# A second routing search of eight rounds with an exactness test, a branch of VectorE alone, and bounds brought into rows by VectorE

## The chip, the cores and the metric

The kernel runs on one core of a Trainium2 chip. Its engines are TensorE (matmuls, in the profile PE, its weight loads PEld), VectorE (DVE), ScalarE (ACT), GpSimd (POOL, here also the queue of gathers and scatters) and SyncE (SP, the queue of all other transfers). The metric is the device time of one execution in microseconds, lower is better; the profile adds one execution taken with the hardware profiler.

## What is computed

Block-causal attention over 8 batches, 8 heads and 576 positions, whose output, as 4608 rows of 512, goes through a mixture of 8 experts. Each expert takes exactly 576 rows, in the order of all logits together:

```python
logits = x @ w_gate                      # 4608 x 8
order = np.argsort(-logits.flatten())
for idx in order:
    tok, e = (int(idx) // E, int(idx) % E)
    if assigned[tok] >= 0 or counts[e] >= cap:
        continue
    assigned[tok] = e
    counts[e] += 1
for e in range(E):
    mask = assigned == e
    out[mask] = np.maximum(x[mask] @ w1[e], 0.0) @ w2[e]
```

The kernel gets the same assignment in eight searches. In each, every row that is left proposes to its best expert that is left; for every expert the 576th largest proposal is found; the expert for which it is highest wins, takes its 576 rows, and both drop out.

## The kernel before

The first half, class Attn, computes the attention and the logits. The second, class Moe, has three kinds of work per expert, all written as generators. `route(k)` is search k: which expert is the k-th, and which rows it takes. `weights(k)` loads that expert's weights on SyncE's queue (L1018) and splits them into two 16-bit parts (ScalarE L1035, L1042, L1046; GpSimd L1048, or VectorE L1037 for part of the first two experts). `gather(k)` fetches the rows by index on GpSimd's queue (L1078); they are turned by a DMA transpose (L1104), those of the first expert by TensorE (L1089). `ffn(k)` is the two layers: h (L1129) in two stretches of rows, each with eight blocks (h_0 to h_7), evacuated by ScalarE into HH (L1115) and by VectorE into HL (L1117); then y (L1155, L1159) in five blocks of rows, y_0 to y_4, evacuated by ScalarE (L1137) and scattered to the output on GpSimd's queue (L1145).

A search (L735 on) narrows a lower bound for every expert in base 4. All proposals lie as PB, one expert to each group of partitions (partition number modulo 8). In round t three candidates per expert are tried, 1, 2 and 3 steps of 4^-t above the bound. VectorE counts the proposals below two of them (L801), ScalarE those of the third by a sum of signs (ja, L770); a small matmul adds the counts over the partitions of one expert (tot, L817); VectorE turns the sums into the next digit (sg, L820). Behind round six the proposals are shifted by the bound (P2, L774), so that later digits keep their precision. After 14 rounds (`NS`) `finish()` adds the last digit (L825, L826); TensorE transposes the bounds, which lie one expert to a partition, into rows that every partition sees (th L831, bc L832); VectorE finds the winner (L835 to L845, the one-hot row oh), its bounds and the rows above them (L849 to L861). `place` numbers the rows by prefix sums and matmuls (po, L903 to L907), `invert` makes a list of indices of them (pe L1005, ps L1012, ix L1014).

The first search (k = 0) already does four rounds only (`NX`), then a test (L885 to L897) whose result TensorE, ScalarE, VectorE and SyncE load into a register (L975). If it is not zero they skip the rounds 4 to 13 (L962).

The order of every engine's instructions is fixed when the program is built: class Sched keeps the generators as tasks, with a cost, a priority and conditions for each step, and lists the step that can start first. Engines run their lists in that order and wait for semaphores, so a matmul that waits for VectorE holds all matmuls behind it. Conditions that matter here: `route(k)` starts when search k-1 is done and y_0 of expert k-2 has begun (`('mid',k-2)`); `gather(k)` waits until expert k-2 is done. Accumulators of h and y are four banks (tag "g"). Index lists, expert numbers and weights hang on the end of a search: `weights(k)` is started from L859, `gather(k)` behind ix.

Of the kernel before, what the change touches and what calls it, by code (L numbers as in the profile page):

```python
# [625 lines left out]
class Moe:  # L626
    def __init__(s,tc,nc,ctx,sc,L,xd,w1,w2,out):
        s.tc,s.nc,s.sc,s.L,s.xd,s.w1,s.w2,s.out=tc,nc,sc,L,xd,w1,w2,out
        s.NT=xd.shape[0]; s.D=w1.shape[1]; s.E=w1.shape[0]; s.F=w1.shape[2]; s.CAP=s.NT//s.E; s.C=s.NT//P
        s.NS=14; s.NSC=6; s.NX=4  # L630
        s.IFE=(mybir.EngineType.Activation,mybir.EngineType.PE,mybir.EngineType.DVE,mybir.EngineType.SP)
        s.cp=ctx.enter_context(tc.tile_pool(name="mcp",bufs=1))
        s.ident=s.cp.tile([P,P],F32,name="mident"); make_identity(nc,s.ident)
        s.am=s.cp.tile([P,8],F32,name="m_am"); s.nam=0; nc.gpsimd.memset(s.am,2.0**-50)
        s.ab=s.cp.tile([P,1],F32,name="m_ab")
        s.vm=s.cp.tile([P,s.C],F32,name="m_vm"); s.nP=s.cp.tile([P,s.C,s.E],F32,name="m_nP"); s.Lr=s.cp.tile([P,s.C,s.E],F32,name="m_Lr")
        s.early=[]; s.W={}; s.X={}; s.ix={}; s.half={}; s.ny=0
# [38 lines left out]
    def pools(s,ctx):  # L676
# [52 lines left out]
    def route(s,k):  # L729
        nc=s.nc; rp=s.rp; C,E=s.C,s.E; V=nc.vector; sc=s.sc  # L730
# [18 lines left out]
        else:  # L749
            if k==0: PB,PV,CB,base=s.first  # L750
            else:
# [11 lines left out]
                CB,base=s.begin(k); sc.busy(D,250)  # L763
# [15 lines left out]
            lo=CB[:,0:1]; nw=s.zero; PBx=PB; wk=s.wk if k else s.sw  # L779
            BC=s.BC[k%2]; f=rp.tile([P,3,8],F32,tag="f",name=f"f{k}"); m1=rp.tile([P,6],F32,tag="m1",name=f"m1{k}"); oh=f[:,1]  # L780
            los,lo2s,hi2s,ei=[m1[:,i:i+1] for i in range(2,6)]; d2=R("d2"); u=rp.tile([P,8],F32,tag="u8",name=f"u8{k}")
            def rounds(t0,t1,live):
                nonlocal lo,nw,PBx,base
                for t in range(t0,t1):
                    w=4.0**-t
                    cnt=rp.tile([P,3],F16,tag="cnt",name=f"cn{k}_{t}")
                    cand=base
                    if t:
                        cand=rp.tile([P,3],F32,tag="cand",name=f"cd{k}_{t}")
                        yield D,70 if k==0 else 210,('P2',k) if PBx is not PB else None  # L790
                        if k==0: V.tensor_tensor(cand[:,2:3],base[:,2:3],nw,op=OP.add)
                        else:
                            for i in (2,0,1): V.tensor_scalar(cand[:,i:i+1],lo,nw,(i+1)*w,op0=OP.add,op1=OP.add)
                    P2=s.P2 if t==s.NSC else None
                    sg=signs(PBx,cand[:,2:3],cnt,t,P2)
                    if live: sc.add(sg,0,sc.now+200); sc.nolat()
                    for i in range(2):
                        yield D,429
                        jk=rp.tile([P,N],F16,tag="jk",name=f"jk{k}_{t}_{i}")
                        if t and k==0: V.scalar_tensor_tensor(jk,base[:,i:i+1].to_broadcast([P,N]),nw,PBx[:,:N],op0=OP.add,op1=OP.is_gt,accum_out=cnt[:,i:i+1])  # L800
                        else: V.tensor_scalar(jk,PBx[:,:N],cand[:,i:i+1],0.0,op0=OP.is_lt,op1=OP.add,accum_out=cnt[:,i:i+1])  # L801
                        if i==0 and live: sc.nolat()
                    add=lambda o,a,b: V.tensor_tensor(o,a,b,op=OP.add) if k==0 else V.tensor_scalar(o,a,b,None,op0=OP.add)
                    if t: add(lo,lo,nw)
                    if P2 is not None:
                        V.tensor_scalar(CB[:,2:3],lo,-1.0,None,op0=OP.mult); sc.set(('nlo',k))
                        lo=CB[:,1:2]; PBx=P2
                    if not live:
                        for _ in sg: pass
                    if t==s.NS-1: add(CB[:,2:3],CB[:,0:1],lo)  # L810
                    elif k==0:
                        base=rp.tile([P,3],F32,tag="base",name=f"bs{k}_{t}")
                        V.tensor_scalar(base,s.io3,wk[:,t+1:t+2],lo,op0=OP.mult,op1=OP.add)
                    if live: sc.busy(D,330 if k==0 else 150)
                    yield T,30,('sg',k,t)
                    tot=s.ps.tile([P,512],F32,tag="tot",name=f"tot{k}_{t}")
                    nc.tensor.matmul(tot[:,0:3],lhsT=s.bo,rhs=cnt,start=True,stop=True)  # L817
                    yield D,72
                    sg=rp.tile([P,4],F32,tag="sg",name=f"sg{k}_{t}")
                    V.scalar_tensor_tensor(sg[:,0:3],tot[:,:3],s.NT-s.CAP+0.5,wk[:,t:t+1].to_broadcast([P,3]),op0=OP.is_le,op1=OP.mult,accum_out=sg[:,3:4])  # L820
                    nw=sg[:,3:4]
                    if live: sc.lag(93)
            def finish():
                yield D,140
                V.tensor_scalar(CB[:,2:3],CB[:,2:3],nw,None,op0=OP.add)  # L825
                V.tensor_scalar(lo,lo,nw,None,op0=OP.add)  # L826
                yield T,90,'rt'
                tk=sc.take()
                ps=s.ps.tile([P,512],F32,tag="rt",name=f"bc{k}")
                th=s.ps.tile([P,512],F32,tag="tot",name=f"th{k}")  # L830
                nc.tensor.transpose(th[:,:32],CB[:32,2:3].to_broadcast([32,P]),s.ident[:32,:32])  # L831
                for i in range(2): nc.tensor.transpose(ps[:,32*i:32*i+32],CB[:32,i:i+1].to_broadcast([32,P]),s.ident[:32,:32])  # L832
                th=th[:,0:8]
                yield D,77
                V.tensor_reduce(m1[:,0:1],th,axis=AX.X,op=OP.max)  # L835
                yield D,138
                V.scalar_tensor_tensor(f[:,0],th,m1[:,0:1],s.wt8,op0=OP.is_equal,op1=OP.mult)
                pb=ps[:,:64].rearrange("p (i x) -> p i x",i=2)[:,:,0:8]
                if k: V.tensor_copy(BC[:,0:2],pb); V.tensor_scalar(BC[:,2],ps[:,32:40],4.0**(1-s.NS),None,op0=OP.add)
                else: V.tensor_scalar(BC[:,0:2],pb,s.gr,None,op0=OP.mult); V.tensor_scalar(BC[:,2],ps[:,32:40],s.gr,4.0**(1-s.NS),op0=OP.mult,op1=OP.add)  # L840
                sc.set(tk)
# [7 lines left out]
                V.tensor_tensor(sm,BC,oh[:,None,:].to_broadcast([P,4,8]),op=OP.mult)  # L849
                V.tensor_tensor(d2,PV,be(oh),op=OP.mult)  # L850
                yield D,670
                V.tensor_reduce(m1[:,2:6],sm,axis=AX.X,op=OP.add)
                V.tensor_reduce(ds_,d2,axis=AX.X,op=OP.add)
                yield D,420
                V.tensor_scalar(MM[:,0],ds_,los,hi2s,op0=OP.subtract,op1=OP.is_gt)
                ge=rp.tile([P,C],F16,tag="ge",name=f"ge{k}")
                V.tensor_scalar(ge,ds_,los,lo2s,op0=OP.subtract,op1=OP.is_ge)
                V.tensor_copy(eidx,ei)
                if k: sc.add(s.weights(k,eidx),1,sc.now)  # L859
                yield D,106  # L860
                V.tensor_tensor(MM[:,1],ge,MM[:,0],op=OP.subtract)  # L861
            if k:
                yield from rounds(0,s.NS,True)
                yield from finish()
            else:
                yield from rounds(0,s.NX,True)
# [356 lines left out]
```

## Time and profile before

| | us |
|---|---|
| median of 3 runs (770.09 to 771.24) | 771.02 |
| the profiled execution | 771.09 |
| its span, first to last instruction | 769.3 |
| TensorE busy in the span | 715.6 |
| VectorE busy | 559.4 |
| ScalarE busy | 536.6 |
| GpSimd busy | 467.8 |

Rows of the timeline and of groups read: start (or none), busy time, engine, line, operation, output<-inputs, shapes, count; in square brackets the engine's idle time before the row and what ended it. Groups end in total busy time, mean nanoseconds of one, and idle time before them. The attention takes the first 340 us. The first expert's layers begin at 361, the second's at 418.5; each later one takes about 50.

### The profile page before, as it was taken

What the parts mean: (1) busy time and instruction counts of PE and PEld (TensorE: products, weight loads), DVE (VectorE), ACT (ScalarE), POOL (GpSimd) and SP (SyncE); (2) the same over time, 40 slices, a digit from 0 to 9 for tenths busy, and PEclk for the clock granted to TensorE, in tenths of its full rate; (3) what the DMA queues carried; (4) which work ended last, traced back from release to release, by engine and by line L of the source; (5) the groups of instructions that cost most, each with busy time, mean ns of one, the idle gap of its engine ahead of it and who ended that gap; (6) DMA issues with size and microseconds to landing.
All of it is one profiled execution on the core that took longest, in us unless ns stands there. A gap on an engine that the chain in (4) does not pass through costs nothing.

```text
span 769.3 us, 19008 instructions
## 1 busy us (share of the span) xinstructions
PE 715.6 (93%) x6516; PEld 474.7 (62%) x6516; DVE 559.4 (73%) x2290; ACT 536.6 (70%) x1451; POOL 467.8 (61%) x515
## 2 busy tenths in 40 slices
PE   5879999999999999966999999999999999999997
PEld 3557776766776777743545747647567475574753
DVE  6899889997799888758988978879687693430210
ACT  5788888988898898844935869594965948393211
POOL 5888978997799876714314448293761926666001
PEclk9999999999999999986999999999999999999999
DMA  9888999999999995266229376482925719853101
GB/s 203 163 160 171 207 187 216 201 168 226 187 210 171 221 196 103 78 124 192 99 74 228 104 247 158 161 211 71 292 76 193 178 43 268 273 139 88 35 14 49
DMA packets 249122, 122.84 MB, mean 160 GB/s; under 512 B 205600, under 2 KB 232096, under 8 KB 249024
## 3 DMA queue, kind: packets, MB, share of 16 engines
q1 hardware_dynamic: 243088, 102.60, 60.2%
q0 software_dynamic: 5936, 19.01, 7.9%
q8 instruction: 52, 0.85, 0.5%
q14 instruction: 46, 0.38, 0.2%
HBM read 71.45 MB, written 18.87 MB: 117 GB/s over the span
## 4 chain that ended last, share of the span: by engine, by line
PE 40%; DMA 5%; issue 4%; POOL 3%; ACT 1%; POOLq 0%; SPq 0%; DVE 0%; ACTq 0%; DVEq 0%
PE h L1129 22%; PE y L1155 15%; DMA raw<-in_moe_w_dram 2%; PE y L1159 2%; POOL xg L1078 2%; POOL W L1048 1%; DMA X<-xg 1%; DMA out_dram<-yo,ix 1%; PE pe L1005 1%; ACT ja L770 1%; DMA xg<-x,ix 0%; PE tot L817 0%; ACT yo L1137 0%; POOL out_dram L1145 0%; ACT raw L1042 0%
## 5 line engine op out<-in xcount | busy, mean ns | idle before, releaser
L442 POOL TENSOR_TENSOR P<-P,m 128x320 f32<-128x320 f32 (+8 forms) x285 | 210.2, 773 | 46.0 <-DVE m L434 30.6
L1129 PE MATMUL h<-X,W 128*128 128x320 f16 (+3 forms) x1536 | 195.4, 286 | 1.6 <-DMA X<-xg 1.6
L1129 PEld LDWEIGHTS <-W 128*128 128x128 f16 x1536 | 141.5, 98 | 43.1 <-issue 3.7
L420 ACT ACTIVATE P<-psb,m 128x576 f32<-128x576 f32 (+8 forms) x288 | 149.7, 548 | 25.6 <-DVE m L413 17.7
L1155 PE MATMUL y<-W,HH 128*128 128x512 f16 x512 | 152.3, 379 | 0.0
L409 DVE TENSOR_REDUCE m<-psb 128x1 f32<-128x576 f32 (+8 forms) x288 | 124.9, 481 | 11.6 <-PE psb L384 11.3
L1048 POOL TENSOR_TENSOR W<-raw,W 128x1024 f16<-128x1024 f32 x56 | 118.3, 2134 | 19.7 <-ACT W L1046 17.3
L467 PE MATMUL psb<-mident,P 128*128 128x128 f32 x800 | 104.6, 278 | 10.4 <-POOL P L442 5.4
L1145 POOL DMA_INDIRECT out_dram<-yo,ix x40 | 39.2, 981 | 118.0 <-ACT yo L1137 73.0
L384 PEld LDWEIGHTS <-qT 128*64 128x64 f16 x1408 | 77.0, 111 | 42.3 <-issue 28.0
L384 PE MATMUL psb<-kT,qT 128*64 128x288 f16 (+8 forms) x704 | 90.8, 284 | 10.8 <-ACT P L420 9.5
L467 PEld LDWEIGHTS psb<-mident,P 128*128 128x128 f32 x800 | 86.3, 141 | 22.0 <-POOL P L442 8.2
L502 PE MATMUL psb<-PT,V 128*64 128x448 f32 (+5 forms) x776 | 97.2, 388 | 0.9 <-DVE PT L450 0.4
L1155 PE MATMUL y<-W,HL 128*128 128x512 f16 x256 | 97.0, 379 | 0.0
L1115 ACT ACTIVATE HH<-h 128x320 f16<-128x320 f32 (+3 forms) x128 | 52.0, 410 | 62.3 <-PE h L1129 57.1
L1078 POOL DMA_INDIRECT xg<-x,ix x40 | 40.9, 1022 | 81.4 <-DMA raw<-in_moe_w_dram 48.5
L448 ACT ACTIVATE PT<-psb 128x512 f32<-128x512 f32 (+1 forms) x165 | 82.7, 595 | 5.3 <-PE psb L467 5.0
L1117 DVE SCALAR_TENSOR_TENSOR HL<-h,HH 128x320 f16<-128x320 f32 (+3 forms) x128 | 57.3, 452 | 37.0 <-ACT HH L1115 36.6
L384 PE MATMUL psb<-kS,qT 128*64 128x288 f16 (+8 forms) x704 | 83.2, 281 | 0.4 <-DVE kS L354 0.2
L1155 PEld LDWEIGHTS <-HH 128*128 128x128 f16 x512 | 46.9, 98 | 52.9 <-issue 1.8
L1042 ACT ACTIVATE raw<-raw 128x512 f32<-128x512 f32 x112 | 67.7, 625 | 9.4 <-DMA raw<-in_moe_w_dram 9.4
L502 PEld LDWEIGHTS psb<-PT,V 128*64 128x64 f32 x776 | 49.5, 137 | 32.2 <-issue 24.3
(241 smaller groups left out, 1035.3 us busy)
## 6 DMA issues: line engine op xcount, KB each, us to landing
raw<-in_moe_w_dram SPq DMA_DIRECT2D x64, 512.0 KB, 5.3
x<-XR SPq DMA_DIRECT2D x8, 1152.0 KB, 5.6
kn<-in_k_dram SPq DMA_DIRECT2D x15, 576.0 KB, 5.0
qn<-in_q_dram SPq DMA_DIRECT2D x15, 576.0 KB, 7.2
V<-in_v_dram SPq DMA_DIRECT2D x64, 128.0 KB, 4.1
V<-in_v_dram SPq DMA_DIRECT2D x16, 64.0 KB, 3.6
xg<-x,ix POOLq DMA_INDIRECT x41, 4.5
out_dram<-yo,ix POOLq DMA_INDIRECT x40, 2.8
```

The source lines that it names most:

```text
L384: nc.tensor.matmul(out if len(K1.shape) == 2 else out.rearrange("p (r j) -> p r j", r=2), lhsT=A[:, h, 64 * i:64 * i + 64], rhs=K1, start= ...
L409: nc.vector.tensor_reduce(m[:, 0, c:c + 1], ps[:, o:o + 64 * (i + 1)] if g else s.part(ps, g, i, o), axis=AX.X if g else AX.XY, op=OP.max)
L420: nc.scalar.activation(out, in_, AF.Exp, bias=m[:, 1, c:c + 1], scale=s.ESC, accum_out=m[:, 2, c:c + 1])
L442: nc.gpsimd.tensor_tensor(sl, sl, m[:, 3, c:c + 1].to_broadcast([P, w]), op=OP.mult)
L448: s.nc.scalar.activation(out, in_, AF.Copy)
L467: nc.tensor.transpose(ps[:, a], s.Pb[n % s.NP][:, s.OFF[i] + 128 * j:s.OFF[i] + 128 * j + P], s.ident)
L502: nc.tensor.matmul(ps[64 * h:64 * h + 64, 64 * (i0 - b0):64 * (b1 - b0)], lhsT=vn[:, j, 2 * (n % 2) + h, :], rhs=pt[:, s.PTI[(j, i0)]:s.PT ...
L1042: nc.scalar.activation(raw[:,x],raw[:,x],AF.Copy,scale=s.WS)
L1048: nc.gpsimd.tensor_tensor(lw,raw,hi,op=OP.subtract)
L1117: nc.vector.scalar_tensor_tensor(HL[:,f,ts],ps,0.0,HH[:,f,ts],op0=OP.max,op1=OP.subtract)
L1129: nc.tensor.matmul(ps,lhsT=W[:,a,d,f*P:f*P+P],rhs=X[:,4*(d//2)+d%2+l,ts],start=(d==0 and n==0),stop=(d==3 and n==2))
L1155: if m<4: nc.tensor.matmul(ps,lhsT=Z[:,f,m*P:m*P+P],rhs=Y[:,a,f],start=(f==n==0),stop=(f==7 and n==2))
```

## The change

The second search (k = 1) stops after eight rounds instead of 14 and does not shift its proposals. Then `early()` adds the last digit, counts the proposals below the bound that has been reached (jx), adds the counts by a matmul (wn), brings the bounds into rows and finds the highest. The test is 1 if one expert alone has the highest bound and exactly 4608 - 576 proposals of it lie below. VectorE alone loads the result into a register and branches: on 1 it skips `general()`, on 0 it does the six rounds that are left, with counting, adding over partitions and spreading all by VectorE itself, and finds the winner again. The other five searches keep 14 rounds.

`heads()` replaces the first part of `finish()`. In searches two to seven (k from 1) the bounds are brought into rows by three VectorE transposes of 128 x 32 in place of the three TensorE transposes; the first search keeps those.

```diff
-        s.NS=14; s.NSC=6; s.NX=4
+        s.NS=14; s.NSC=6; s.NX=4; s.EX={1:8}
...
-                    P2=s.P2 if t==s.NSC else None
+                    P2=s.P2 if t==s.NSC and not (live and k in s.EX) else None
...
-            def finish():
-                yield D,140
-                V.tensor_scalar(CB[:,2:3],CB[:,2:3],nw,None,op0=OP.add)
-                V.tensor_scalar(lo,lo,nw,None,op0=OP.add)
-                yield T,90,'rt'
...
+            def heads():
+                if k:
+                    th=rp.tile([P,3,32],F32,tag="th3",name=f"th{k}"); s.th3=th
+                    yield D,300
+                    for i in (2,0,1): V.transpose(th[:,i],CB[:,i:i+1].to_broadcast([P,32]))
+                    pb,th=th[:,0:2,0:8],th[:,2,0:8]
+                else:
+                    yield T,90,'rt'
...
+            def general():
+                z,zt,rs,x,tt=[rp.tile([P,w],F32,name=f"{n}_g{k}",bufs=1) for n,w in (("z",32),("zt",32),("rs",8),("x",32),("tt",32))]
...
+                for t in range(s.EX[k],s.NS):
...
+                    for i in range(3):
+                        cd=rp.tile([P,1],F32,name=f"cd_g{k}_{t}_{i}",tag="cdg"); jk=rp.tile([P,N],F16,tag="jk",name=f"jkg{k}_{t}_{i}")
+                        V.tensor_scalar(cd,lo,(i+1)*4.0**-t,None,op0=OP.add)
+                        V.tensor_scalar(jk,PBx[:,:N],cd,0.0,op0=OP.is_lt,op1=OP.add,accum_out=z[:,i:i+1])
+                    V.transpose(zt,z)
+                    V.tensor_reduce(rs,zt.rearrange("p (a e) -> p e a",e=8),axis=AX.X,op=OP.add)
+                    for b in range(4): V.tensor_copy(s4[:,b],rs[32*b:32*b+32])
+                    V.tensor_reduce(s1,s4.rearrange("p b e -> p e b"),axis=AX.X,op=OP.add)
+                    for b in range(4): V.tensor_copy(x[32*b:32*b+32].rearrange("p (a e) -> p a e",e=8),s1[:,None,:].to_broadcast([32,4,8]))
+                    V.transpose(tt,x)
...
+                for _ in heads(): pass
+            def early():
+                yield D,70
+                V.tensor_scalar(CB[:,2:3],lo,nw,None,op0=OP.add)
+                yield D,429
+                cx=rp.tile([P,1],F16,name=f"cx{k}",tag="cx"); jk=rp.tile([P,N],F16,tag="jk",name=f"jx{k}")
+                V.tensor_scalar(jk,PB[:,:N],CB[:,2:3],0.0,op0=OP.is_lt,op1=OP.add,accum_out=cx)
+                V.tensor_scalar(lo,lo,nw,None,op0=OP.add)
+                yield T,60
+                wn=s.ps.tile([P,512],F32,tag="tot",name=f"wn{k}")[:,0:8]
+                nc.tensor.matmul(wn,lhsT=cx.to_broadcast([P,P]),rhs=s.bo[:,0:8],start=True,stop=True)
+                yield from heads()
...
+                V.tensor_scalar(u8,s.th3[:,2,0:8],m1[:,0:1],0.0,op0=OP.is_equal,op1=OP.add,accum_out=n1[:,0:1])
+                V.tensor_scalar(u8,oh,n1[:,0:1],1.0,op0=OP.mult,op1=OP.is_equal)
+                yield D,90
+                V.scalar_tensor_tensor(u8,wn,float(s.NT-s.CAP),u8,op0=OP.is_equal,op1=OP.mult,accum_out=n1[:,1:2])
+                rl=nc.alloc_registers(f"exact{k}",engines=(mybir.EngineType.DVE,))
+                nc.engines[mybir.EngineType.DVE].reg_load(rl.handles[0],n1[0:1,1:2].bitcast(I32))
+                rv=nc.snap(rl,donate=True)
+                more=s.tc.If(rv==0,preferred_fallthrough_block=False); more.__enter__()
+                general()
+                more.__exit__(None,None,None)
+                sc.busy(D,1500)
+            def finish():
+                if k in s.EX: yield from early()
+                else:
+                    yield D,140
+                    V.tensor_scalar(CB[:,2:3],CB[:,2:3],nw,None,op0=OP.add)
+                    V.tensor_scalar(lo,lo,nw,None,op0=OP.add)
+                    yield from heads()
...
-                yield from rounds(0,s.NS,True)
+                yield from rounds(0,s.EX.get(k,s.NS),True)
```

The built orders show where this lands. On TensorE, in the first expert's first layer, up to the matmul of round seven (tot_7) both programs are alike. Before, the six rounds tot_8 to tot_13 follow among h_4 to y_0, then th and bc, then po in the middle of y_1:

```order
L1129 MATMUL h_4_1_6213<-X_5764,W_0_5762 128x448
L817 LDWEIGHTS m_bo
L817 MATMUL tot_8_6224<-cn_8_6196,m_bo 128x3
...
L817 MATMUL tot_13_6373<-cn_13_6353,m_bo 128x3
...
L831 MATMUL th_6386<-mident,CB_5791 128x32
L832 MATMUL bc_6385<-mident,CB_5791 128x32 x2
...
L903 MATMUL po_2_6449<-m_sh,m_ones 128x72
```

In the change the count wn stands at the place of tot_8, TensorE's own part of the branch is a jump among the matmuls of h_5, and po comes within h_7 (39 matmuls behind wn):

```order
L1186 MATMUL h_4_1_6206<-X_5764,W_0_5762 128x448
L881 LDWEIGHTS cx_6202
L881 MATMUL wn_6216<-m_bo,cx_6202 128x8
...
L1186 MATMUL h_5_1_6234<-X_5764,W_0_5762 128x448
L894 UNCONDITIONAL_BRANCH
...
L960 MATMUL po_2_6502<-m_sh,m_ones 128x72
```

So po, and with it pe, ps and the index list, moves ahead by more than a block of the second layer.

On VectorE, behind the digit of round seven (sg_7), a further round follows before (its candidates cd_8 and counts jk_8):

```order
L820 SCALAR_TENSOR_TENSOR sg_7_6194<-tot_7_6189,m_wk 128x3
L793 TENSOR_SCALAR cd_8_6197<-CB_5791,sg_7_6194 128x1 x3
L801 TENSOR_SCALAR jk_8_0_6207,cn_8_6196<-m_P_5257,cd_8_6197 128x288
L801 TENSOR_SCALAR jk_8_1_6210,cn_8_6196<-m_P_5257,cd_8_6197 128x288
L803 TENSOR_SCALAR CB_5791<-CB_5791,sg_7_6194 128x1
```

In the change the test, the load of the register and the branch stand there, with two evacuations HL between:

```order
L820 SCALAR_TENSOR_TENSOR sg_7_6194<-tot_7_6188,m_wk 128x3
L874 TENSOR_SCALAR CB_5791<-CB_5791,sg_7_6194 128x1
L1174 SCALAR_TENSOR_TENSOR HL_5850<-h_2_1_6144,HH_5849 128x448
L877 TENSOR_SCALAR jx_6203,cx_6202<-m_PB,CB_5791 128x288
...
L1174 SCALAR_TENSOR_TENSOR HL_5850<-h_3_1_6175,HH_5849 128x448
L827 STREAM_TRANSPOSE th_6218<-CB_5791 128x32 x3
L838 TENSOR_REDUCE m_5804<-th_6218 128x1
...
L888 SCALAR_TENSOR_TENSOR x_6239,x_6240<-wn_6216,x_6239 128x8
L890 TENSOR_LOAD x_6240
L894 COMPARE_AND_BRANCH
L894 UNCONDITIONAL_BRANCH
```

Behind the branch come sm and d of the ranking and HL of h_4 and h_5. On GpSimd's queue the scatters of the first expert's output (out_dram) stood ahead of the gathers (xg):

```order
L1145 DMA out_dram<-yo_0_6410,ix_5390 4608x512
L1145 DMA out_dram<-yo_1_6490,ix_5390 4608x512
L1078 DMA xg_0_6560<-x,ix_6440 128x1024
L1078 DMA xg_1_6579<-x,ix_6440 128x1024
L1078 DMA xg_2_6597<-x,ix_6440 128x1024
```

and now two gathers come first:

```order
L894 UNCONDITIONAL_BRANCH
L1135 DMA xg_0_6618<-x,ix_6490 128x1024
L1135 DMA xg_1_6643<-x,ix_6490 128x1024
L1202 DMA out_dram<-yo_0_6645,ix_5390 4608x512
L1135 DMA xg_2_6665<-x,ix_6490 128x1024
```

The searches behind it move ahead against the layers: tot_0 of the third search stood in y_2 of the first expert and stands in y_1, tot_0 of the fourth moves from y_2 of the second expert to its y_0.

More of the change, by code (lines that the diff above doesn't have):

```diff
@@ L822, in rounds @@
                     if live: sc.lag(93)
-            def finish():
-                yield D,140
-                V.tensor_scalar(CB[:,2:3],CB[:,2:3],nw,None,op0=OP.add)
-                V.tensor_scalar(lo,lo,nw,None,op0=OP.add)
-                yield T,90,'rt'
[L828 to L833, printed above, removed]
+            def heads():
[6 more added lines that the diff above has]
+                    yield T,90,'rt'
+                    tk=sc.take()
+                    ps=s.ps.tile([P,512],F32,tag="rt",name=f"bc{k}")
+                    th=s.ps.tile([P,512],F32,tag="tot",name=f"th{k}")
+                    nc.tensor.transpose(th[:,:32],CB[:32,2:3].to_broadcast([32,P]),s.ident[:32,:32])
+                    for i in range(2): nc.tensor.transpose(ps[:,32*i:32*i+32],CB[:32,i:i+1].to_broadcast([32,P]),s.ident[:32,:32])
+                    pb,th=ps[:,:64].rearrange("p (i x) -> p i x",i=2)[:,:,0:8],th[:,0:8]
                 yield D,77
@@ L837, in finish @@
                 V.scalar_tensor_tensor(f[:,0],th,m1[:,0:1],s.wt8,op0=OP.is_equal,op1=OP.mult)
[L838 to L841, printed above, removed]
+                if k: V.tensor_copy(BC[:,0:2],pb); V.tensor_scalar(BC[:,2],pb[:,1],4.0**(1-s.NS),None,op0=OP.add)
+                else: V.tensor_scalar(BC[:,0:2],pb,s.gr,None,op0=OP.mult); V.tensor_scalar(BC[:,2],pb[:,1],s.gr,4.0**(1-s.NS),op0=OP.mult,op1=OP.add); sc.set(tk)
                 yield D,77
@@ L845, in finish @@
                 V.tensor_scalar(oh,f[:,0],m1[:,1:2],None,op0=OP.is_equal)
+            def general():
+                z,zt,rs,x,tt=[rp.tile([P,w],F32,name=f"{n}_g{k}",bufs=1) for n,w in (("z",32),("zt",32),("rs",8),("x",32),("tt",32))]
+                s4=rp.tile([32,4,8],F32,name=f"s4_g{k}",bufs=1); s1=rp.tile([32,8],F32,name=f"s1_g{k}",bufs=1)
+                lo,PBx=CB[:,0:1],PB
+                V.memset(z,0.0); V.memset(CB[:,1:2],0.0)
+                for t in range(s.EX[k],s.NS):
+                    if t==10:
+                        V.tensor_scalar(CB[:,2:3],lo,-1.0,None,op0=OP.mult)
+                        V.tensor_scalar(s.P2[:,:N],PB[:,:N],CB[:,2:3],None,op0=OP.add)
+                        lo,PBx=CB[:,1:2],s.P2
+                    for i in range(3):
[8 more added lines that the diff above has]
+                    V.transpose(tt,x)
+                    sg=rp.tile([P,4],F32,tag="sg",name=f"sgg{k}_{t}")
+                    V.scalar_tensor_tensor(sg[:,0:3],tt[:,:3],s.NT-s.CAP+0.5,s.wk[:,t:t+1].to_broadcast([P,3]),op0=OP.is_le,op1=OP.mult,accum_out=sg[:,3:4])
+                    V.tensor_scalar(lo,lo,sg[:,3:4],None,op0=OP.add)
+                V.tensor_scalar(CB[:,2:3],CB[:,0:1],CB[:,1:2],None,op0=OP.add)
+                for _ in heads(): pass
@@ new lines, in early @@
+            def early():
[9 more added lines that the diff above has]
+                yield from heads()
+                u8=rp.tile([P,8],F32,tag="x8",name=f"x8{k}"); n1=rp.tile([P,2],F32,tag="x1",name=f"x1{k}")
+                yield D,250
+                V.tensor_scalar(u8,s.th3[:,2,0:8],m1[:,0:1],0.0,op0=OP.is_equal,op1=OP.add,accum_out=n1[:,0:1])
[9 more added lines that the diff above has]
+                sc.busy(D,1500)
```

## The prediction

> **What bounds the kernel now.** I read the page first: span, then the chain that ended last.
>
> ```profile
> span 769.3 us, 19008 instructions
> ...
> PE 40%; DMA 5%; issue 4%; POOL 3%; ACT 1%; POOLq 0%; SPq 0%; DVE 0%; ACTq 0%; DVEq 0%
> ```
>
> The chain is TensorE with a few percent of transfers, and VectorE has 0% of it. A change that shortens VectorE's routing therefore pays only where TensorE really stands still, or where it takes matmuls off TensorE. So I cut the second half into stretches (columns: busy microseconds of PE, PEld, DVE, ACT, POOL, then granted clock, DMA share, GB/s).
>
> ```profile
> 360.00:418.50 58.50, 53.27 (x423) 28.93 (x421) 51.00 (x248) 35.51 (x86) 19.94 (x15) 1.00 0.46 129
> 418.50:740.00 321.50, 320.35 (x2436) 201.50 (x2436) 202.72 (x997) 208.59 (x488) 169.67 (x114) 1.00 0.55 155
> ```
>
> From 418.5 to 740 TensorE idles 321.50 - 320.35 = **1.15 us** in 321, at full clock. From 360 to 418.5, while the first expert's layers and the second search run side by side, it idles 5.2. Most of that lies before 370, ahead of round five of the second search, where the new program is the same. What is left at the end of this stretch is one wait, in the list of waits, in the chain and (last row) in the timeline of TensorE:
>
> ```profile
> PE h L1129 <- DMA X<-xg: 1.6, 1, 1.6
> ...
> 405.05 3.71 DMA xg<-x,ix
> ...
> 410.15 8.32 DMA X<-xg
> ...
> 418.51 1.80 PE L1129 MATMUL h<-X,W 128*128 128x256 f16 x15 [1.56 <-DMA X<-xg]
> ```
>
> The second expert's rows are gathered from 405.05 and turned by DMA; TensorE gets them at 418.51, after 1.56 us of idle. From the first gather to the first matmul it is 13.5 us. This is the one place where the second search is late.
>
> **The change part by part.** The profiled execution took 771.09 us, 1.8 more than its span; the median of the runs is 771.02. The sum is made against 771.09.
>
> *Six rounds go.* The row of a round's matmul, and how often it ran:
>
> ```profile
> 380.47 0.18 PE L817 MATMUL tot<-cn,m_bo 128*128 128x3 f16 x1
> 380.50 2.43 PE L1129 MATMUL h<-X,W 128*128 128x448 f16 x12
> 382.77 0.17 PE L817 MATMUL tot<-cn,m_bo 128*128 128x3 f16 x1
> ...
> L817 PE MATMUL tot<-cn,m_bo 128*128 128x3 f16 x88 | 15.0, 171 | 8.6 <-DVE jk L800 4.2 <-DVE jk L801 2.6 <-ACT ja L770 1.5
> ```
>
> 88 = 4 + 6 x 14: the first search passed its own test after four rounds, the six others ran fourteen. Rounds of the second search are 2.3 us apart (382.77 - 380.47), but a round costs TensorE only 0.03 to 0.04 us (380.47 to 380.50), since twelve matmuls of the first layer lie between. Six rounds less, one count matmul more: **-0.2 us** of TensorE. Their length on VectorE, 13 us, is worth only what waits for the search.
>
> *What waits: X.* The new order puts the second search's pe and ps matmuls into y_0 instead of y_2, and gathers start before the first output. In matmuls: po stands 39 of 448 columns after the count, 0.19 us each (2.27 / 12), so 382.8 + 7.4 = 390.2; then three of these, fifteen of y at 0.22, the pe block, six of y: indices at about 397, against 404.6. Two gathers go first, then an output that has to wait for y_0 to about 399. By the 13.5 us above the rows are there at 411, while TensorE arrives near 416. **-1.56 us**, with 5 us to spare; neither more nor less, since expert two's weights are also asked earlier and nothing else waits there.
>
> *Bounds into rows by VectorE, in searches two to seven.* TensorE loses th and bc:
>
> ```profile
> 394.69 0.38 PE L1155 MATMUL y<-W,HL 128*128 128x512 f16 x1
> 395.00 0.24 PE L831 MATMUL th<-mident,CB 32*128 32x32 f32 x1
> ...
> 395.29 0.61 PE L1155 MATMUL y<-W,HH 128*128 128x512 f16 x2
> 395.73 0.38 PE L1155 MATMUL y<-W,HL 128*128 128x512 f16 x1
> 395.94 0.59 PE L1155 MATMUL y<-W,HH 128*128 128x512 f16 x2
> ...
> 440.29 1.38 PE L1129 MATMUL h<-X,W 128*128 128x320 f16 x9
> 441.61 0.24 PE L831 MATMUL th<-mident,CB 32*128 32x32 f32 x1
> ...
> 441.89 0.99 PE L1129 MATMUL h<-X,W 128*128 128x320 f16 x6
> ...
> 442.72 0.59 PE L1155 MATMUL y<-W,HH 128*128 128x512 f16 x2
> ...
> L831 PE MATMUL th<-mident,CB 32*128 32x32 f32 x6 | 1.4, 238 | 0.0
> ```
>
> In the second layer a step is 0.21 (395.73 to 395.94); across the transposes it is 0.60 (394.69 to 395.29): 0.39 lost. In the first layer six steps take 0.83, 0.138 each; nine would take 1.24 and took 1.60: 0.36 lost. Six times 0.37 is **-2.2 us**, the largest term, and certain work on the bounding engine. VectorE gets three small transposes for it and stops waiting for TensorE.
>
> *The test, the load and the branch on VectorE.* First what stands ahead of them, then the load and the branch of the first search, which has the same form:
>
> ```profile
> 380.77 0.08 DVE L820 DVE_READ_ACCUMULATOR sg<-tot,m_wk 128x1 f32 x1
> 391.46 0.61 DVE L1117 SCALAR_TENSOR_TENSOR HL<-h,HH 128x448 f16<-128x448 f32 x1
> 395.27 0.17 DVE L835 TENSOR_REDUCE m<-th 128x1 f32<-128x8 f32 x1 [0.40 <-PE th L831]
> ...
> 396.22 0.19 DVE L849 TENSOR_TENSOR sm<-m_BC,f 128x32 f32<-128x32 f32 x1
> ...
> 397.95 0.35 DVE L892 TENSOR_TENSOR_SCAN SC<-m_ones,MM 128x36 f16<-128x36 f16 x2
> ...
> L801 DVE TENSOR_SCALAR_CACHE_REDUCE jk<-m_P,cd 128x288 f16<-128x288 f32 x84 | 39.6, 509 | 0.0
> L762 DVE STREAM_TRANSPOSE m_PB<-PV 128x32 f32<-128x32 f32 x6 | 1.2, 206 | 0.1
> ```
>
> ```profile
> 349.31 0.20 DVE L895 TENSOR_SCALAR_CACHE_REDUCE f<-tx,m 128x8 f32<-128x8 f32 x1
> ...
> 349.99 0.08 DVE L897 DVE_READ_ACCUMULATOR f<-wn,f 128x1 f32 x1
> 350.78 0.59 PE L978 MATMUL warm<-m_iom,m_ones 128*128 128x512 f16 x1 [1.15 <-DVE L L923]
> ...
> 354.18 0.23 PE L1012 MATMUL ps<-ixt,m_b 128*32 128x5 f16 x8 [1.01 <-DVE ixt L1008]
> 354.48 0.17 DVE L1014 CAST ix<-ps 128x5 int32<-128x5 f32 x1 [0.34 <-PE ps L1012]
> 354.88 1.04 PE L978 MATMUL warm<-m_iom,m_ones 128*128 128x512 f16 x2 [0.46 <-PEq L962]
> 355.38 0.46 DVE L754 TENSOR_TENSOR m_nP<-L,m_vm 128x288 f32<-128x288 f32 x1 [0.74 <-DVEq L962]
> ```
>
> Round seven's digit is there at 380.85. Behind it: two HL at 0.61, the count 0.6, two additions and three transposes at 0.21, the heads 0.95 (395.27 to 396.22), the test 0.76 (349.31 to 350.07); some 4.4 with small overlaps, 385.2. The load: TensorE had its flag at 350.07 and went on at 350.78, so 0.71, an upper bound. The branch: 0.74 of idle VectorE, an upper bound too. So 386.7, then 2.1 to the end of the prefix scan (396.22 to 398.30) and two HL between, 1.1: **389.9**, against 390.2 where TensorE stands at po. It just fits: **0**. The ends are 0 and, with load and branch both a whole microsecond longer, about 1.7. Queued behind the branch are HL of h_4 to h_7 and the ranking; who waits are po and, later, y_0's accumulator, which h_4's HL must free by 390.8 and does at 388.
>
> The other engines each pass one unconditional branch. TensorE's lies between two matmuls of h_5; nearest row: 0.46 idle, with a compare in it and nothing to run ahead. Bounds 0 and 0.46; I take **+0.1**, near the lower end because matmuls are already queued ahead of it. ScalarE, GpSimd and SyncE have idle time here.
>
> [...]
>
> ```profile
> q8 instruction: 52, 0.85, 0.5%
> ```
>
> 52 blocks of 16 KB took 0.5% of 16 x 769.3 us, 62 us, so about 1.2 us of transfer each. The first search's jumps, over some hundred instructions, show 0.46 and 0.74 in all, so no such load was in them; the general path is as long. [...]
>
> *Later searches.* They begin up to 10 us earlier against the layers, so three more experts get the pattern that the fourth and fifth have now: all ten early rounds beside the second layer, where ScalarE also converts weights. That pattern's price now:
>
> ```profile
> PE tot L817 <- ACT ja L770: 0.8, 2, 0.7
> ```
>
> This list is from 420 on. Bounds: all 1.15 us of idle gone, or 0.8 more in each of three experts, +2.4. The conversions on GpSimd also move ahead of the first output, which helps; I take **+0.6**, nearer to what stands there now.
>
> Sum: -0.2 - 1.56 - 2.2 + 0 + 0.1 + 0.6 = -3.3; 771.09 - 3.3 = **767.8 us**. Ends: -0.2 - 1.56 - 2.2 - 1.15 = -5.1, 766.0; with +0.46 and +2.4, -1.1, 770.0.
>
> **The rivals.**
>
> *ScalarE becomes the bound in the second layers.* Each of three experts more pays 0.8 to 1.2 in rounds that wait behind a late weight: 769 to 771. For it: the wait above already exists. Against it: it is 0.8 in two experts, with TensorE 99.6% busy. I set 769.4.
>
> [...]
>
> *Everything fits.* TensorE's idle time after 418.5 goes as well: 766.0.
>
> *The branch is not skipped, and the kernel is slower.* Then VectorE alone does six rounds: three counts of 0.6, two transposes, and about sixteen small operations near 0.2, 4 to 5 us a round, with the repeated heads some 26 us, while TensorE stands at po from 390.2: 767.8 + 26 = 794. It decides whether the eighth round's bound separates exactly 576 proposals. On the reference's inputs it does: divided by the power of two that the kernel scales by, the 576th and 577th largest proposals of the winning expert (2) are 0.2945636 and 0.2945485, the bound after round eight is 0.2945557, and 4032 = 4608 - 576 lie below; no other expert shares the bound. The margin is 7e-6 of values near 0.3, so only a computed logit off by that would undo it.
>
> **How the numbers follow.** A measurement of this kernel can tell about 0.2%, 1.5 us, from no change: faster is below 769.5, slower above 772.6. Chances: forecast 0.55, ScalarE 0.22, loaded code 0.08, all fits 0.09, branch not skipped 0.06. Faster: 0.54 + 0.08 + 0.06 + 0.09 = 0.77. Same: 0.01 + 0.11 + 0.02 = 0.14. Slower: 0.03 + 0.06 = 0.09. The range goes from 766.0 to 770.2: it takes in the forecast with both ends, the fetch, the full fit and over half of the ScalarE case, and leaves out the general path.
>
> **What would show it.** L831 and L832 gone for six searches, and neighbouring matmuls 0.21 and 0.138 apart there; L817's count down from 88 to 82; no TensorE wait for X near 417; no instruction of the general path. VectorE's idle time at the branch near 1.5 us; a wait of TensorE for MM or SC at po would show it longer. Waits of TensorE for ja between 440 and 620 above 0.8 us would show the ScalarE rival. I am wrong if TensorE's busy time does not fall by over 2 us, or if its idle time after 418 passes 3 us.

## The result, and the profile after

The changed kernel takes **798.57 us** (median of 4 runs, 797.9 to 800.5) against 771.13 of before in the same comparison: the ratio is 1.0356 (95% interval 1.0327 to 1.0385). Forecast were 767.8 us, faster. The profiled execution of the changed kernel took 798.14 us. Its page, first the span, then the chain that ended last:

```profile
span 796.0 us, 18928 instructions
...
PE 37%; DVE 7%; DMA 3%; ACT 2%; issue 1%; SPq 0%; POOLq 0%; DVEq 0%; ACTq 0%
PE y L1212 19%; PE h L1186 14%; DVE m_nP L754 2%; PE y L1216 2%; DMA raw<-in_moe_w_dram 2%; DVE PV L756 1%; ACT raw L1099 1%; DVE HL L1174 1%; DMA xg<-x,ix 1%; DVE jk L801 1%; PE pe L1062 1%; ACT W L1103 1%; DVE cd L793 0%; ACT HH L1172 0%; DMA out_dram<-yo,ix 0%
```

VectorE, with 0% of the chain before, now has 7%; 3% of it are L754 and L756, the first two large instructions of a search, the rest is spread over many lines. TensorE's list of waits from 340 on (microseconds in total, times, longest), then the groups of L754, L756, L760 and L817 (after), and L754 and L756 of before (last two rows):

```profile
PE rt L760 <- DVE PV L756: 22.9, 3, 7.7
```

```profile
L754 DVE TENSOR_TENSOR m_nP<-L,m_vm 128x288 f32<-128x288 f32 x6 | 19.9, 3324 | 0.8 <-DVEq L1019 0.7
L756 DVE SCALAR_TENSOR_TENSOR PV<-m_nP,L 128x288 f32<-128x288 f32 x6 | 11.1, 1856 | 0.2
L760 PE MATMUL rt<-mident,PV 128*128 128x128 f32 x12 | 3.4, 379 | 22.9 <-DVE PV L756 22.9
L817 PE MATMUL tot<-cn,m_bo 128*128 128x3 f16 x82 | 14.1, 171 | 8.9 <-DVE jk L800 4.2 <-DVE jk L801 2.8 <-ACT ja L770 1.3
```

```profile
L756 DVE SCALAR_TENSOR_TENSOR PV<-m_nP,L 128x288 f32<-128x288 f32 x6 | 2.7, 458 | 0.2
L754 DVE TENSOR_TENSOR m_nP<-L,m_vm 128x288 f32<-128x288 f32 x6 | 2.7, 456 | 0.8 <-DVEq L962 0.7
```

The code of L754 and L756 is the same, the shapes are the same, and the mean of one went from 0.46 to 3.3 and 1.9 us. TensorE waited three times, 22.9 us in all, for PV. The timeline around the first of the three (all engines but weight loads; columns as before):

```profile
492.42 0.46 DVE L754 TENSOR_TENSOR m_nP<-L,m_vm 128x288 f32<-128x288 f32 x1
492.91 8.85 DVE L756 SCALAR_TENSOR_TENSOR PV<-m_nP,L 128x288 f32<-128x288 f32 x1
...
493.08 8.36 POOL L1105 TENSOR_TENSOR W<-raw,W 128x1024 f16<-128x1024 f32 x4
...
501.91 0.66 PE L760 MATMUL rt<-mident,PV 128*128 128x128 f32 x2 [7.56 <-DVE PV L756]
...
502.36 1.06 PE L1212 MATMUL y<-W,HH 128*128 128x512 f16 x2
...
507.51 0.84 PE L1212 MATMUL y<-W,HH 128*128 128x512 f16 x2
...
508.40 0.59 PE L1212 MATMUL y<-W,HH 128*128 128x512 f16 x2
```

An instruction of 0.46 us is on record with 8.85: not as a wait ahead of it, but as busy time. Beside it GpSimd runs four subtractions of the next weights (L1105) without a pause, 493.08 to 501.44; VectorE ends 0.3 us later, at 501.76. The second and third time it is L754 (8.93 us at 552.58, 9.19 us at 611.79), each beside a run of four. What else it costs is in the stretches (busy microseconds of PE, PEld, DVE, ACT, POOL, then granted clock, DMA share, GB/s):

```profile
493.00:502.50 9.50, 1.94 (x10) 0.95 (x8) 9.33 (x8) 1.93 (x5) 8.42 (x5) 0.75 1.08 248
502.50:508.50 6.00, 6.00 (x18) 2.19 (x17) 2.57 (x14) 3.66 (x9) 0.00 (x0) 0.54 0.19 42
508.50:515.00 6.50, 6.50 (x35) 2.89 (x34) 4.35 (x28) 6.25 (x14) 5.29 (x4) 1.00 0.11 42
```

After 7.56 us of idle TensorE does not come back at its speed: 18 matmuls in 6 us at a granted clock of 0.54, then 35 in 6.5 at 1.00. The slow steps reach to about 507.6, some 5.7 us from the first matmul at 501.91 (two matmuls of y take 1.06 at first, 0.84 at 507.51, 0.59 at 508.40). Behind the second and third wait, of 7.65 and 7.64 us, they last some 3.9 and 5.7 us, and the granted clock is 0.50 both from 561.7 to 565.6 and from 621.2 to 626.9.

The second search itself went as forecast:

```profile
385.26 0.08 DVE L888 DVE_READ_ACCUMULATOR x<-wn,x 128x1 f32 x1
...
386.51 0.19 DVE L906 TENSOR_TENSOR sm<-m_BC,f 128x32 f32<-128x32 f32 x1 [1.17 <-DVEq L894]
...
389.04 0.18 DVE L918 TENSOR_TENSOR MM<-ge,MM 128x36 f16<-128x36 f16 x1
...
389.23 0.20 PE L960 MATMUL po<-m_sh,m_ones 128*128 128x72 f16 x1
```

No row of the general path is there: the branch was skipped, load and branch together took 1.17 us of VectorE, and the sums for po were ready as TensorE reached it.

### The profile page after: what moved, and what is told of

Its sections match the earlier page's. It is cut to its first block, busy times and chain, and to the rows that moved or that the text cites. A ratio compares the mean times of both kernels' runs of the same rounds, so it can differ in the third digit from the quotient of the medians.

```text
span 796.0 us, 18928 instructions
## 1 busy us (share of the span) xinstructions
PE 719.4 (90%) x6493; PEld 475.1 (60%) x6493; DVE 587.1 (74%) x2253; ACT 533.8 (67%) x1438; POOL 466.9 (59%) x515
## 4 chain that ended last, share of the span: by engine, by line
PE 37%; DVE 7%; DMA 3%; ACT 2%; issue 1%; SPq 0%; POOLq 0%; DVEq 0%; ACTq 0%
PE y L1212 19%; PE h L1186 14%; DVE m_nP L754 2%; PE y L1216 2%; DMA raw<-in_moe_w_dram 2%; DVE PV L756 1%; ACT raw L1099 1%; DVE HL L1174 1%; DMA xg<-x,ix 1%; DVE jk L801 1%; PE pe L1062 1%; ACT W L1103 1%; DVE cd L793 0%; ACT HH L1172 0%; DMA out_dram<-yo,ix 0%
## 5 line engine op out<-in xcount | busy, mean ns | idle before, releaser
L1212 PE MATMUL y<-W,HH 128*128 128x512 f16 x512 | 157.6, 390 | 0.0
L1105 POOL TENSOR_TENSOR W<-raw,W 128x1024 f16<-128x1024 f32 x56 | 118.1, 2133 | 14.9 <-ACT W L1103 13.6
L1212 PE MATMUL y<-W,HL 128*128 128x512 f16 x256 | 99.5, 389 | 0.0
L1212 PEld LDWEIGHTS <-HH 128*128 128x128 f16 x512 | 48.0, 100 | 52.9 <-issue 4.5
L1103 ACT ACTIVATE W<-raw 128x512 f16<-128x512 f32 x112 | 69.2, 626 | 0.0
```

The source lines that it names most:

```text
L1103: nc.scalar.activation(hi[:,x],raw[:,x],AF.Copy)
L1105: nc.gpsimd.tensor_tensor(lw,raw,hi,op=OP.subtract)
L1212: if m<4: nc.tensor.matmul(ps,lhsT=Z[:,f,m*P:m*P+P],rhs=Y[:,a,f],start=(f==n==0),stop=(f==7 and n==2))
```

## The experiments

Two theories to begin with. **A**: VectorE's instruction with two inputs in SBUF is held by GpSimd's subtractions, which also read SBUF, until GpSimd's run is over. **B**: VectorE is held by something else of the new order (the branch, a semaphore, the transposes), and the subtractions stand beside it by chance. The rows above show the two side by side, and VectorE's end 0.3 us behind GpSimd's; that the one causes the other is so far the author's estimate, and the first two runs below test it. All times are beside the kernel before on the same chip, where it took 771.3 to 771.6 us in the median; single runs of it lay between 768.2 and 777.0.

**e1_psum: the same instructions, with one input in PSUM.** vm and nP of the searches from the third on lie in a PSUM bank.

```diff
         vm,nP=s.vm,s.nP
+        if k>1 and not last:
+            pp=s.ps.tile([P,512],F32,tag="xt",name=f"np{k}",bufs=2); vm,nP=pp[:,288:288+C],pp[:,:288].rearrange("p (c e) -> p c e",e=E)
```

> The changed kernel, with the mask nP and the row maxima vm of searches three to seven in PSUM instead of SBUF; nothing else moves on any engine. Theory A (VectorE instructions with two SBUF inputs stand still while GpSimd runs its weight subtractions, which read SBUF too): L754 and L756 then have one SBUF input, all twelve take 0.4 to 0.6 us instead of up to 9.2, TensorE's waits for PV at L760 (22.9 us) go, and with them the half-clock stretches behind them (about 2.7 us each): 765 to 769 us. Theory B (these two instructions are long because their data, or something that they depend on, come late: gathers, or the order of the searches): unchanged, 797 to 800 us.

Measured: 773.5 us (771.34 to 777.04, 10 runs), ratio 1.0029 (1.0005 to 1.0053), a little slower than before. The timeline of VectorE and GpSimd in the sixth search (k = 5; L1107 is the subtraction):

```profile
543.29 2.15 POOL L1107 TENSOR_TENSOR W<-raw,W 128x1024 f16<-128x1024 f32 x1
...
543.36 0.46 DVE L756 TENSOR_TENSOR np<-L,np 128x288 f32<-128x288 f32 x1
543.85 0.46 DVE L758 SCALAR_TENSOR_TENSOR PV<-np,L 128x288 f32<-128x288 f32 x1
```

Here the collision in time is still there: both stand wholly inside the first subtraction, and both take 0.46 us. Only the place of an input differs: the branch, the transposes and the order of the searches are those of the changed kernel. B falls. The gain that A's expectation hoped for on top did not come.

**e2_wait: the subtractions wait until PV is written.** GpSimd copies one column of the next search's PV ahead of the first subtraction, so that it waits for L756.

```diff
...
-                yield G,2079
+                yield G,2079,('pv',k+1) if 1<k<s.E-2 and n<4 else None
+                if 1<k<s.E-2 and k not in s.pd: s.pd.add(k); nc.gpsimd.tensor_copy(s.pj,s.pv[k+1][:,0,0:1])
```

> The changed kernel with nP and vm left in SBUF; before the first of expert k's weight subtractions (k = 2 to 5) GpSimd copies one column of PV of search k+1, so that the subtractions start behind L756. The gathers stay where they are. Theory A: L754 and L756 at 0.46 us again, TensorE's waits at L760 below 2 us in all, 766 to 770 us. Theory B with the gathers as the cause: the gathers still run beside L754 and L756, so these stay at 8 to 9 us somewhere and the time stays above 790.

Measured: 770.58 us (769.48 to 774.3, 10 runs), ratio 0.9988 (0.9962 to 1.0014). Its rows at the place of the first collision:

```profile
493.31 0.46 DVE L754 TENSOR_TENSOR m_nP<-L,m_vm 128x288 f32<-128x288 f32 x1
493.87 0.46 DVE L756 SCALAR_TENSOR_TENSOR PV<-m_nP,L 128x288 f32<-128x288 f32 x1
...
494.40 0.18 POOL L1105 COPY m_pj<-PV 128x1 f32<-128x1 f32 x1 [0.42 <-DVE PV L756]
494.56 2.12 POOL L1106 TENSOR_TENSOR W<-raw,W 128x1024 f16<-128x1024 f32 x1
```

GpSimd gives up 0.4 to 1.0 us, three times, and 28 us of the whole are back. So the collision of these two groups is all of the loss against before, as far as these times can tell. Long instructions of VectorE remain in this trace (the fourteen prefix scans at L949 take 10.4 us, where two of them take 0.35 at 437.13, so about 8 us of it by estimate is standing; in the changed kernel one took 8.30 beside a run of four subtractions from 672.38), but TensorE has no wait for them.

**e3_heads and e4_early: each half of the change alone.** e3 keeps 14 rounds in the second search, and only the bounds come into rows by VectorE. e4 has the short second search, and TensorE brings the bounds into rows.

```diff
 e3_heads
-        s.NS=14; s.NSC=6; s.NX=4; s.EX={1:8}
+        s.NS=14; s.NSC=6; s.NX=4; s.EX={}
 e4_early
-                if k:
+                if k in s.EX:
                     th=rp.tile([P,3,32],F32,tag="th3",name=f"th{k}"); s.th3=th
...
```

> Only the part of the change that brings bounds into rows by VectorE; the second search does all 14 rounds without a test or a branch. If the term of the prediction is right, six times 0.37 us of TensorE go: 768 to 769.5 us. Theory A adds that it is as fast as that only if no search's L754 or L756 falls beside a run of subtractions; GpSimd's order here puts the five gathers and at most three subtractions ahead of y_0's scatter, so one collision of up to 6 us can be seen, 769 to 777. Theory B' (the VectorE transposes themselves make later two-input instructions slow): long L754 or L756 in most searches, over 785.

> Only the other part: second search of eight rounds with the test and the branch, VectorE's transposes for that search alone; searches three to seven keep the TensorE transposes. Theory A: the searches still move ahead against GpSimd's subtractions, so long L754 or L756 stay (three or four of them), 785 to 803 us. Theory B': with the transposes gone the long instructions go, 768 to 772.

Measured: e3 770.89 us, ratio 0.9996 (0.9974 to 1.0019); e4 771.46 us, 0.9996 (0.9971 to 1.0021). The 768 to 769.5 hoped for of e3 did not come. Neither has a long L754 or L756, which I had not expected of e4. Its rows show why:

```profile
494.65 0.46 DVE L754 TENSOR_TENSOR m_nP<-L,m_vm 128x288 f32<-128x288 f32 x1
494.79 1.11 POOL L1136 DMA_INDIRECT xg<-x,ix  x1 [0.30 <-issue]
495.14 0.46 DVE L756 SCALAR_TENSOR_TENSOR PV<-m_nP,L 128x288 f32<-128x288 f32 x1
...
495.92 2.14 POOL L1106 TENSOR_TENSOR W<-raw,W 128x1024 f16<-128x1024 f32 x1
```

L756 ends at 495.60, 0.32 us ahead of the subtraction. In before the distance in the same search was 7 us (L756 to 497.88, the first subtraction at 505.04, with five gathers and an output between). So half of the change already moves the subtractions up to the edge, and the other half pushes them over it. Is it that near? The next run asks.

**e6_push: e4, and VectorE 1.1 us later.**

```diff
...
+                if 3<k<7:
+                    for _ in range(6): V.tensor_scalar(s.pz,vm,1.0,None,op0=OP.mult)
                 V.tensor_tensor(nP,Lm,b3(vm),op=OP.is_lt)
```

> The kernel of e4_early (only the shorter second search; TensorE brings the bounds into rows), which had no long instruction, with six one-input instructions of VectorE (128x36, about 0.18 us each, 1.1 us in all) ahead of L754 in searches k=4 to 6. They do nothing else. In e4_early L756 of k=4 ended at 495.60, 0.32 us ahead of GpSimd's run of four subtractions at 495.92; the delay is longer than that margin. Theory (a collision decided by tenths of a microsecond): at least L754 or L756 of k=4 takes 6 to 9 us, TensorE waits 6 us or more for it, and as the later ones then slip too, two or three collide: 780 to 803 us. Rival (the long instruction needs the transposes on VectorE, or something else of the full change): all L754 and L756 stay at 0.46 and the run takes 770 to 774 us.

Measured, in one execution: 802.87 us, TensorE waits three times, 25.3 us. One microsecond more of work costs 31. In two of the three, though, it was neither nP nor PV (L754 and L756, here L756 and L758) that stood, as the expectation had it (first the timeline, then the line's list: durations of one, lowest, median, highest):

```profile
495.21 10.12 DVE L755 TENSOR_SCALAR m_pz<-m_vm 128x36 f32<-128x36 f32 x6
505.23 0.45 DVE L756 TENSOR_TENSOR m_nP<-L,m_vm 128x288 f32<-128x288 f32 x1
...
L755 DVE TENSOR_SCALAR m_pz<-m_vm x18: 182/183/9029, 495.2 to 625.4; 128x36 f32<-128x36 f32 x18
```

In each of these two, one of the delaying instructions, with a single input, stood for about 9 us (9.03 the longest). So two inputs are not needed, and A was worded too narrowly.

**e5_gap and e9_long_gap: does VectorE get in between two subtractions?** A memset on GpSimd, which reads nothing, stands ahead of every subtraction: of 128x1 in e5, of 128x512 in e9.

```diff
...
                 yield G,2079
+                nc.gpsimd.memset(s.pj,0.0)
```

> The changed kernel, with a one-column memset on GpSimd ahead of every one of its subtractions, so that no two of them follow one another directly. [...] Rival 'held to the end': a short instruction between is not enough, the longest is still 8 to 10 us, and the run takes 795 to 802 us.

> As e5_gap, but the memset between GpSimd's subtractions writes 128x512 f32, some 0.5 us by the rows of GpSimd's other memsets (about 1 ns an element), and reads nothing. In e5_gap the memset took 0.11 us and lay under the end of the subtraction before it, so GpSimd was never without a reading instruction for long. [...] Rival 'held until GpSimd's queue stops for a semaphore or a transfer': still 9 to 11 us long (four subtractions and three memsets), 797 to 808 us.

Measured, in one execution each: e5 801.45 us, e9 792.25. In both VectorE stood to the end of the run. The rows of e5, then of e9 (its second collision, in the seventh search):

```profile
496.01 9.01 DVE L756 SCALAR_TENSOR_TENSOR PV<-m_nP,L 128x288 f32<-128x288 f32 x1
...
502.52 0.11 POOL L1105 MEMSET m_pj<- 128x1 f32 x1
502.57 2.13 POOL L1106 TENSOR_TENSOR W<-raw,W 128x1024 f16<-128x1024 f32 x1
```

```profile
605.70 0.54 POOL L1105 MEMSET m_pj<- 128x512 f32 x1
605.71 10.55 DVE L756 SCALAR_TENSOR_TENSOR PV<-m_nP,L 128x288 f32<-128x288 f32 x1
...
606.19 2.14 POOL L1106 TENSOR_TENSOR W<-raw,W 128x1024 f16<-128x1024 f32 x1
...
613.82 2.11 POOL L1106 TENSOR_TENSOR W<-raw,W 128x1024 f16<-128x1024 f32 x1
```

Half a microsecond without a reading instruction, three times, did not let VectorE in: VectorE ends at 616.26, GpSimd at 615.93. By the author's estimate VectorE would, if it got in behind the first subtraction, have stood for 2 to 3 us, and the runs would have taken 769 to 778 us; both came out otherwise, and what the rows show is "held to the end of the run". In its fifth search (k = 4) e9 had no collision: the first memset put the first subtraction at 495.19, and L756 had ended at 495.02. So it had two collisions and not three, which fits the 9 us between it and e5.

**e7_wait_again, e8_heads_again, e10_before: what is left without the collision.** The kernels of e2, of e3 and of before once more, unchanged.

> The kernel of e2_wait once more (the changed kernel, where GpSimd's first subtraction waits for PV of the next search), for a second trace and a narrower interval. Theory 'the gains are real, the collision alone ate them': from the first matmul of h of the first expert to the last of y it takes 399 to 400.5 us, against 402.99 in the trace of before (764-361), as in e2_wait (399.48), and the ratio of times is 0.994 to 0.998 (766.5 to 770). Rival 'the gains go elsewhere': that stretch takes 402 us or more in this trace, and the ratio lies within 0.998 to 1.002.

> The kernel of e3_heads once more (only the bounds into rows by VectorE; the second search keeps 14 rounds), since its profiled execution had a late transfer of 4.4 us. Theory (the transposes are 2.2 us of TensorE): without such a wait the stretch from the first matmul of h to the last of y takes 400.3 to 401.3 us, against 402.99, TensorE waits 1 to 2 us for ja, and the ratio is 0.996 to 0.999. Rival (TensorE waits as long for VectorE or ScalarE as the transposes took): 402 to 404 us in that stretch, ratio 0.999 to 1.002. All L754 and L756 at 0.46 us in both.

> The kernel before, unchanged, for a second trace of it and for what its times do by chance. If traces of one kernel vary as the two of e2_wait did (399.9 and 403.5 us from the first matmul of h to the end of the last of y), the stretch lies anywhere within 400 to 406 us, TensorE's wait for the second expert's rows (X) is between 0 and 5 us, and the ratio of times is 1.000 within 0.002. If instead the first trace of before is typical, it is 403.4 within 0.5 us with 1.6 us of wait for X, and then the 3.5 us that e2_wait and e8_heads_again showed in that stretch are gains.

Measured: e7 770.13 us (769.04 to 775.07, 12 runs), ratio 0.9983 (0.9965 to 1.0001); e8 771.29, 1.0008 (0.9985 to 1.0031); e10 772.4, 1.0004 (0.9981 to 1.0026). The traces, from the first matmul of h to the end of the last of y (the first column is the stretch, the second its length, the third TensorE's busy time): before, e10, e2, e7, e8, e4, and the changed kernel.

```profile
360.93:764.30 403.37, 397.03 (x2966) 240.58 (x2965) 254.23 (x1244) 246.79 (x578) 192.47 (x133) 1.00 0.51 144
...
362.37:764.45 402.08, 397.33 (x2966) 239.84 (x2965) 253.73 (x1244) 246.45 (x578) 191.17 (x132) 1.00 0.51 144
...
362.50:762.36 399.86, 394.86 (x2943) 239.65 (x2942) 256.47 (x1207) 243.42 (x565) 192.27 (x136) 1.00 0.50 145
...
361.28:764.80 403.52, 396.91 (x2943) 241.13 (x2942) 258.13 (x1207) 243.41 (x565) 193.33 (x137) 1.00 0.50 144
...
360.93:760.76 399.83, 394.76 (x2948) 239.73 (x2947) 255.39 (x1262) 246.14 (x578) 191.64 (x132) 1.00 0.52 145
...
360.61:765.22 404.61, 396.77 (x2958) 240.47 (x2957) 248.84 (x1192) 244.17 (x565) 192.35 (x132) 1.00 0.50 144
...
360.55:791.06 430.51, 402.64 (x2943) 241.65 (x2942) 282.14 (x1207) 244.09 (x565) 192.60 (x133) 0.97 0.46 135
```

One and the same kernel took 399.86 us (e2) and 403.52 (e7) in this stretch, so the theory of e7 (399 to 400.5) held in one trace of two, and e7's ratio, 0.9983, lies just inside its rival's range. e8's stretch (399.83) came out below its theory's 400.3 to 401.3, but its times fell to the rival; e10's 402.08, with no wait for X, lies inside its wide range. A single trace can't tell 3 us here; the times of many runs can. By those of e2 and e7 the change without its collision saves 0.7 to 1.4 us, within 0.2% and not settled as a gain (both intervals reach 1); e1, which takes the collision away by the other means, is 2.2 us slower than before. The change without its collision beats the changed kernel by 28 us and can't be told from before.

## Why the prediction was wrong

**The step that failed is the term "Later searches".** It took the move of the later searches for a question of ScalarE (+0.6, bounds -1.15 and +2.4) and put the move of GpSimd's work down as help: "The conversions on GpSimd also move ahead of the first output, which helps". That move is the loss. A search's result now comes earlier, and with it the gathers and the subtractions of its weights: at the place of the first collision the first gather moved from 5.1 us behind the start of y_0 (497.73 against 492.67) to 5.1 us ahead of it (487.10 against 492.24). But the next search still begins no earlier than y_0 (L754 at 492.42). So the subtractions of one search came to stand beside L754 and L756 of the next, and TensorE's rt, behind PV, holds the whole second layer. The account between the changed kernel and e2 closes: the stretches differ by 430.51 - 399.86 = 30.65; TensorE's three waits are 22.9, and its matmuls take 402.64 - 394.86 = 7.8 longer at the lower clock, 2.6 for each wait; together 30.7. The 7.8 lie where they should: the matmuls of y at L1212 are busy for 257.1 us, and for 249.2 at the same line in e2 and in e7. (Against e7's whole stretch the account is 3.7 us smaller: that trace had a granted clock of 0.90 and 0.76 in its first two stretches of 5 us, and longer waits for transfers.) The prediction's own signs of being wrong both came: TensorE's busy time in this stretch rose by 5.6 us, and its idle time behind 418.5 went from 1.15 to 23.2 us (up to 766.5).

I could have seen the risk: L754 reads two tiles in SBUF (L and vm), and the order moves GpSimd's subtractions ahead of the first output. In the trace of before nothing of the kind stood in these two lines (0.45 to 0.46 each), since the subtractions came 3 to 7 us or more after them. But the same hold stands in that trace at another place, in the last search:

```profile
661.23 4.47 DVE L921 TENSOR_SCALAR h<-q 128x36 f16<-128x36 f32 x1
661.44 4.21 POOL L1048 TENSOR_TENSOR W<-raw,W 128x1024 f16<-128x1024 f32 x2
```

The other seven of this line took 0.18 us; this one, with a single input, stood to the end of a run of two subtractions. TensorE had matmuls of y to do and did not wait, so the list of waits does not name it. So the hold was there to be read; that it would meet the path was not.

The other steps:

- *Six rounds go* (-0.2, and +0.1 for TensorE's branch): right. The count of L817 fell from 88 to 82. TensorE's busy time in e4 is 0.26 lower, which also holds one search's transposes and is no more than the 0.30 between the two traces of before. And 39 matmuls of h run from wn to po without a gap, so the branch cost TensorE nothing that can be seen.
- *Bounds into rows by VectorE* (-2.2): the transposes are gone, and TensorE's busy time goes from 397.03 to 394.76 in e8, 2.27 less; in the trace of e3, the same kernel, it is 395.97, 1.06 less, so the size is shown in one trace of two. In the times of e3 and e8 it doesn't appear (ratios 0.9996 and 1.0008).
- *What waits: X* (-1.56): the wait is gone, but it was mis-sized. The second trace of before has no such wait, and in e3, with that part of the order as before, X waits took 4.9 us in one execution and in e8 0.9. It depends on transfers that vary from run to run.
- *Test, load and branch* (0): right. The load and the branch took 1.17 us against 1.45 assumed. (The upper bound of this term, 1.7, was left out of the sum's upper end; with it that end is 771.7 and not 770.0, still far below what was measured.) The second search had its own small collision, which took up part of the slack: L840 stood 1.71 us instead of 0.23 beside one subtraction, with th now in SBUF; in the third search it stood 1.17:

```profile
382.01 0.39 DVE L827 STREAM_TRANSPOSE th<-CB 128x32 f32<-128x32 f32 x3
382.03 2.13 POOL L1105 TENSOR_TENSOR W<-raw,W 128x1024 f16<-128x1024 f32 x1 [0.96 <-ACT W L1103]
382.32 0.12 DVE L838 TENSOR_REDUCE m<-th 128x1 f32<-128x8 f32 x1
382.48 1.71 DVE L840 SCALAR_TENSOR_TENSOR f<-th,m,m_wt 128x8 f32<-128x8 f32 x1
```

- *The rivals*: the general path was skipped, and no late load of code shows (load and branch took 1.17 us in all; 51 blocks against 52). That a jump waits for code, to which the forecast gave 0.08 and which its range takes in as "the fetch", no run here shows. ScalarE as a bound may be there in part: TensorE's wait for ja is 1.5 us in both traces of before, and 2.1, 2.9 and 4.5 in e2, e7 and e4. The forecast's +0.6 is the low end of that. But e3 and e8, again one kernel, have 3.6 and 1.1, so part of the difference is chance. The rival that ended slower had the wrong mechanism; the true one was not among them.

How much of the -3.3 is real without the collision stays open between about 0 and 2.9 us, by the intervals of e2 and e7: the waits for ja and for X may eat it, but no run separates these from the spread of the times.

## What to carry over

When a change moves work on GpSimd, look at which VectorE instructions will stand beside it: on one side the list of those that read two SBUF tiles, as L754 and L756 do (8.85 to 9.19 us here instead of 0.46), or that, like L755 and L921, scale one tile from SBUF to SBUF (9.03 and 4.47 instead of 0.18), on the other the runs of GpSimd's subtractions, and the distance between them in microseconds. If VectorE's side is on the path, fix the order with a wait (770.58 us in e2, against 798.57), or put one of two inputs into PSUM (773.5 in e1); 0.3 us of luck is not an order. And an instruction whose "busy" time grows without a change of its shape may be standing, as here: compare the shortest and the longest of a line within the trace of before, and its means between two profiles, before reading any list of waits.

## What was not expected of the hardware

- The hold lasted as long as GpSimd's run of subtractions, not one instruction: 8.36 us of four subtractions gave 8.85 to 9.19 us, 4.21 of two gave 4.47, 2.13 of one gave 1.71 to an instruction that began inside it. Memsets between, of 0.11 or 0.5 us, didn't end it (9.01 and 10.55).
- VectorE's row starts 0.17, 0.25 and 0.52 us ahead of GpSimd's (492.91 and 493.08 at the first collision, 611.79 and 612.31 at the third) and still loses; the third would by its usual 0.46 us have ended 0.06 us ahead of GpSimd's row. The instructions that had ended 0.32 us ahead in e4 and 0.17 us ahead in e9 went free. By these rows a VectorE instruction that has begun isn't safe, unless the starts of two engines' rows are off by so much; no run here settles which.
- Three transposes and a reduction of VectorE from SBUF ran beside the same subtraction undisturbed (L827 and L838 above, 0.39 and 0.12 us; over all searches the median of one is 0.17 and 0.15).
